# Rounded halves of Q and K loaded by a casting DMA of GpSimd in an attention and feed-forward kernel

## The chip, the cores and the metric

The kernel runs on one core of a Trainium2 chip. The metric is the time of one execution on the device, in microseconds (us). The engines are TensorE (PE; its weight loads are listed as PEld), VectorE (DVE), ScalarE (ACT), GpSimd (POOL) and SyncE (SP, which here only issues DMAs). Each engine runs its own instruction list strictly in order. An instruction that waits for a semaphore holds back all that stands behind it on that engine.

## The reference, cut to what matters

```python
# q, k, v: (8, 8, 576, 64) float32; f: (8, 8, 576)
scores = (1 / sqrt(64)) * q @ k.T
cum = cumsum(log(clip(f, 1e-4, 1)), axis=-1)
decay = cum[:, :, :, None] - cum[:, :, None, :]
attn = softmax(where(causal, -1e9, scores + decay))
x = (attn @ v).transpose(0, 2, 1, 3).reshape(8 * 576, 512)
h = x @ w_in                                   # 512 -> 2048
g = maximum(h, 0) + alpha * minimum(h, 0)
out = g @ w_out                                # 2048 -> 512
```

There are eight batches of eight heads, then a feed-forward layer over 4608 tokens.

## The kernel before, in words

**Pairs.** Two heads of a batch are worked on together, one in partitions 0 to 63 and one in 64 to 127. That makes 32 pairs, numbered n = 0 to 31, four to a batch. For each pair TensorE makes scores in tiles of 128 rows; VectorE adds the decay and the mask (tile `Z`, and `Zt` for the last 64 rows) and takes the row minimum of the negated scores; ScalarE takes the exponential; TensorE transposes the result (line 507), and then multiplies it by the values `vr`. The quotients go through `R`, `rd` and `ri`; VectorE multiplies (line 688), ScalarE rounds the product into `xx` (line 690), and GpSimd puts the remainder beside it (line 692).

**Split numbers.** The TensorE works here on numbers rounded to a shorter format (FP32R). To keep precision, a float32 operand is split into a rounded high half and a low half, the remainder, and a product becomes three products: high by high, high by low, low by high. From pair 4 on (`NN = 4`), Q and K are split so: `load_n` loads `rq` and `rk` (lines 423 and 424, issued by SP), ScalarE copies each to `Qh` and `Kh` (line 462; the write rounds), and GpSimd subtracts, `Ql = rq - Qh` and `Kl = rk - Kh` (line 463). The four halves lie in one buffer of the ring `rQ`, of which there are two. A buffer comes free when the scores of its pair are done, so the halves of pair n can be made once the scores of pair n - 2 are through. Pairs 0 to 3 use the whole float32 numbers.

**What else GpSimd does.** For each pair it prepares `Z` and `Zt` (lines 437, 438, 439, 454) after their loads, and it makes the low halves of `xx` (line 692) and, in the first 160 us, of the 16 columns of `w_in` (line 318, two instructions for each column, which is called fc 0 to fc 15 here). ScalarE (lines 305 and 317) and VectorE (lines 308 to 313) make the high halves of those columns.

**The first matrix product of the feed-forward layer** (`ffn1`) runs between the attention work. For each batch there are 16 columns, each with two halves of six products `bank<-xx,wi`. The first half of a column needs `xx` of the batch's pairs 0 and 1, the second half that of its pairs 2 and 3. The second product of the layer begins after all of it, at about 700 us.

**What sets the order.** The program order on each engine is found when the kernel is built, by a planner (`Plan.run`): each operation is given an engine, an assumed duration, a key and its dependencies. Again and again the planner takes the operation that can start earliest by its own clock, and among those of one engine the one with the lower key. An operation on the engine "-" takes time but no engine. The chip then runs the lists as they are: a wrong assumption shows as a wait. `o_scan` is the prefix sum at about 6 us; `dq` is empty for pair 0 and `[o_scan]` for the others; `kl` and `kc` are keys, the first lower.

Of the kernel before, what the change touches and what calls it, by code (L numbers as in the profile page):

```python
# [13 lines left out]
AF = mybir.ActivationFunctionType  # L14
# [3 lines left out]
B, H, S, D = 8, 8, 576, 64  # L18
# [5 lines left out]
QW = 640  # L24
# [58 lines left out]
class Plan:  # L83
# [5 lines left out]
    def op(self, eng, ns, fn, key, deps=(), bufs=(), two=False, kb=0.0):  # L89
        o = Op()  # L90
        o.eng, o.ns, o.fn, o.key, o.bufs, o.two, o.kb = eng, ns / 1000.0 * SLACK.get(eng, 1.0), fn, key, bufs, two, kb
        o.outs, o.ready, o.end, o.n = [], 0.0, None, 0
        for b in bufs:
            b.left += 1
        for d in deps:
            if d is not None and d.end is None:
                d.outs.append(o)
                o.n += 1
            elif d is not None:
                o.ready = max(o.ready, d.end + self.lag(d, o))  # L100
        self.ops.append(o)
        return o
# [83 lines left out]
def attention_moe(  # L186
# [14 lines left out]
    pe, ve, ac, po, sy = nc.tensor, nc.vector, nc.scalar, nc.gpsimd, nc.sync  # L201
# [3 lines left out]
    op = plan.op  # L205
# [63 lines left out]
    def c_mm(n):  # L269
        return max(110, 13.3 + 0.4175 * n)  # L270
# [7 lines left out]
    def c_act(n):  # L278
        return 65 + n / 1.2

    def c_acs(n):
        return 115 + n / 1.2
# [10 lines left out]
    def c_po(n):  # L293
        return 60 + 2.3 * n
# [26 lines left out]
    def mm(o, lhsT, rhs, start, stop):  # L321
        pe.matmul(o, lhsT, rhs, start=start, stop=stop)  # L322
# [92 lines left out]
    def load_n(n, held):  # L415

        b, p = divmod(n, NP)
        first = n == 0
        kl, kc, bh = NS * n - 16, NS * n - 7, b * H + 2 * p
        bq, bk, bZ = Buf(rrq), Buf(rrk), Buf(rZ)  # L420
        kq = -99 if first else -59 if n == 1 else kl
        dq = [] if first else [o_scan]
        l_q = op("SP", 450, lambda: sy.dma_start(bq.t, qq[b, p]), kq, dq, [bq], kb=320)
        l_k = op("SP", 450, lambda: sy.dma_start(bk.t, kk[b, p]), kq, dq, [bk], kb=288)
        Z, Zt = (lambda: bZ.t[0]), (lambda: bZ.t[1])
        rz = []
        for h in range(2):
            if first:
                bz_ = Buf(rH)
                up = op("PE", 4 * c_mm(512), lambda h=h, bz_=bz_: mm(bz_.t, row()[:, h], ft()[:, 0:512], True, True), -60 + h, o_8 + [o_row], [bft, brow, bz_])  # L430
                got = [op("ACT", c_act(512), lambda h=h, bz_=bz_: ac.activation(Z()[:, h, 0:512], bz_.t, AF.Copy), -60, [up], [bz_, bZ])]
            else:
                got = [op("SP", 400, lambda h=h: sy.dma_start(Z()[:, h, 0:512], c8[bh + h : bh + h + 1, 0:512].broadcast_to([128, 512])),
                          kl + 1, [o_c8], [bZ], kb=256)]
            z4 = lambda h=h: Z()[:, h].rearrange("p (j s) -> p j s", s=128)
            tb = lambda k: tri.rearrange("p (k s) -> p k s", k=1).broadcast_to([128, k, 128])
            m1 = op("POOL", c_po(128 * 3), lambda z4=z4: po.tensor_tensor(z4()[:, 6:9], z4()[:, 0:3], tb(3), ALU.add), kc + 0.1, got + [o_mask], [bZ])  # L437
            m2 = op("POOL", c_po(128), lambda z4=z4: po.tensor_tensor(z4()[:, 3], z4()[:, 3], tri, ALU.add), kc + 0.2, got + [o_mask], [bZ])
            m3 = op("POOL", c_po(128) / 2, lambda z4=z4: po.tensor_copy(z4()[:, 4], z4()[:, 1]), kc + 0.2, got, [bZ])
            rz.append([m1, m2, m3])  # L440
        if first:
            bz2 = [Buf(rH), Buf(rH)]
            cut = ((0, 512), (512, S))

            def up2():
                for b_, (a0, a1) in zip(bz2, cut):
                    mm(b_.t[:, 0 : a1 - a0], row()[:, 2], ft()[:, a0:a1], True, True)

            up = op("PE", 4 * c_mm(512) + 440, up2, -58, o_8 + [o_row], [bft, brow] + bz2)
            tz = [op("ACT", c_act(a1 - a0), lambda b_=b_, a0=a0, a1=a1: ac.activation(Zt()[:, a0:a1], b_.t[:, 0 : a1 - a0], AF.Copy), -58, [up], [b_, bZ])  # L450
                  for b_, (a0, a1) in zip(bz2, cut)]
        else:
            tz = [op("SP", 400, lambda h=h: sy.dma_start(Zt()[64 * h : 64 * h + 64], c8[bh + h : bh + h + 1].broadcast_to([64, S])), kl + 1, [o_c8], [bZ], kb=147) for h in range(2)]
        rt = op("POOL", 260, lambda: po.tensor_tensor(Zt()[:, 512:576], Zt()[:, 512:576], tri2, ALU.add), kc + 0.3, tz + [o_mask], [bZ])
        if n < NN:
            held += [bq, bk]
            return [l_q, l_k], rz, rt, bZ, [(lambda: bq.t, lambda: bk.t)]
        bQ = Buf(rQ)
        Qh, Ql, Kh, Kl = ((lambda j=j: bQ.t[j]) for j in range(4))
        out = []  # L460
        for hi, lo, raw, ld, w in ((Qh, Ql, bq, l_q, QW), (Kh, Kl, bk, l_k, S)):
            o1 = op("ACT", c_acs(w), lambda hi=hi, raw=raw: ac.activation(hi(), raw.t, AF.Copy), kc, [ld], [raw, bQ])  # L462
            o2 = op("POOL", c_po(w), lambda hi=hi, lo=lo, raw=raw: po.tensor_tensor(lo(), raw.t, hi().bitcast(F32), ALU.subtract), kc, [o1], [raw, bQ])  # L463
            out += [o1, o2]
        held.append(bQ)
        return out, rz, rt, bZ, [(Qh, Kh), (Qh, Kl), (Ql, Kh)]
# [3 lines left out]
    def attention(n):  # L470
# [6 lines left out]

        held = []
        rdy, rz, rt, bZ, terms = load_n(n, held)
        bv = Buf(rvr)  # L480
        l_v = op("SP", 400, lambda: sy.dma_start(bv.t, vv[b, p]), kl + 1, [o_scan], [bv], kb=320)
# [361 lines left out]
    for c in (0, 2):  # L843
        bt_ = Buf(rhr)
        tv = lambda bt_=bt_: bt_.t.rearrange("p c j t -> p c (j t)")
        ld = op("SP", 400, lambda c=c, tv=tv: sy.dma_start(tv(), xt[c : c + 2].rearrange("c p t -> p c t")), 1e6, [o_change] + xt_ops, [bt_], kb=512)
# [228 lines left out]
```

## Time and profile before

| | |
|---|---|
| median of 3 runs | 1083.31 us (1081.6 to 1084.06) |
| the profiled execution | 1082.03 us |
| its span, first to last instruction | 1080.2 us |
| mean granted TensorE clock | 0.997 |
| DVE busy | 707.3 us (65%) |
| ACT busy | 699.5 us (65%) |
| POOL busy | 279.4 us (26%) |
| moved by DMA | 170.57 MB, mean 158 GB/s |

The lines of the trace give a start and a duration in us, then the engine, the line of the kernel, the operation, its output and inputs by the names of their buffers with the partitions and elements, and a count where several are merged. In square brackets stands how long the engine was idle just before, and what ended that. SPq is the DMA queue of SP. Matmuls are pipelined and their ends are modelled.

### The profile page before, as it was taken

To read this page: it belongs to the slowest core of one execution; us is meant where nothing else is said; L and a number is where in the kernel's file an instruction comes from. 1 tells how busy PE (TensorE), PEld (TensorE's weight loads), DVE (VectorE), ACT (ScalarE), POOL (GpSimd) and SP (SyncE) were. 2 spreads that over 40 slices of the span, in tenths; PEclk is the share of its full clock that TensorE was granted. 3 is DMA by queue.
4 is the path that set the end of the run, shared out by engine and by line. 5 is a ranking of instruction groups with operands and counts; after the bars stand their busy time and mean duration, and the time that the engine had idled before them with its cause. 6 is when DMAs were issued, how large, how long until landed. Compare 5 with 4: busy or idle time off the path is not lost.

```text
span 1080.2 us, 20892 instructions
## 1 busy us (share of the span) xinstructions
PE 1068.2 (99%) x7428; PEld 910.8 (84%) x7428; DVE 707.3 (65%) x1632; ACT 699.5 (65%) x1638; POOL 279.4 (26%) x407
## 2 busy tenths in 40 slices
PE   8899999999999999999999999999999999999998
PEld 4577777777777777777787888899999999999998
DVE  6896745434434434434433497879989898989994
ACT  6898888967857857857846376656454554646551
POOL 6596774542443433433401000000000000000000
PEclk9999999999999999999999999999999999999999
DMA  6877766663653663553531566563433533443511
GB/s 184 252 221 239 241 193 180 191 182 115 184 174 118 179 181 115 177 177 115 151 104 71 166 221 233 193 206 117 150 126 118 157 118 120 139 134 125 147 61 39
DMA packets 116337, 170.57 MB, mean 158 GB/s; under 512 B 16626, under 2 KB 62601, under 8 KB 116233
## 3 DMA queue, kind: packets, MB, share of 16 engines
q1 hardware_dynamic: 115945, 169.05, 50.2%
q8 instruction: 58, 0.95, 0.4%
q14 instruction: 46, 0.38, 0.1%
q10 hardware_dynamic: 288, 0.20, 0.1%
HBM read 120.68 MB, written 48.52 MB: 157 GB/s over the span
## 4 chain that ended last, share of the span: by engine, by line
PE 96%; DVE 1%; DMA 1%; ACT 0%; POOL 0%; issue 0%; DVEq 0%
PE bank L322 87%; PE bank L507 8%; DMA wr<-in_w_in_dram 1%; PE bank L382 1%; DMA Zt<-c 0%; PE bank L646 0%; PE bank L571 0%; DVE xs L688 0%; ACT es L494 0%; DVE wa L313 0%; POOL Z L437 0%; DVE wa L312 0%; DVE e L527 0%; DVE eT L502 0%; DVE es L624 0%
## 5 line engine op out<-in xcount | busy, mean ns | idle before, releaser
L322 PE MATMUL bank<-xx,wi 128*128 128x512 f32 x1728 | 421.3, 396 | 0.3 <-DVE st L624 0.3
L322 PEld LDWEIGHTS bank<-xx,wi 128*128 128x128 f32 x1728 | 316.7, 188 | 63.3 <-issue 1.9
L770 DVE SCALAR_TENSOR_TENSOR hs<-bank,sa,hs 128x512 f32<-128x512 f32 x96 | 72.0, 750 | 156.6 <-ACT hs L768 156.6
L503 ACT ACTIVATE eT<-bank 128x384 f32<-128x384 f32 x240 | 109.2, 487 | 27.1 <-PE bank L507 23.7
L322 PE MATMUL bank<-wot,xx 128*128 128x256 f32 x1008 | 123.9, 284 | 0.0
L322 PE MATMUL bank<-wi,xx 128*128 128x256 f32 x1008 | 123.9, 284 | 0.0
L322 PEld LDWEIGHTS bank<-wi,xx 128*128 128x128 f32 x1008 | 122.3, 192 | 0.0
L322 PEld LDWEIGHTS bank<-wot,xx 128*128 128x128 f32 x1008 | 122.3, 192 | 0.0
L768 ACT ACTIVATE hs<-bank,ab 128x512 f32<-128x512 f32 x96 | 66.0, 687 | 81.0 <-PE bank L322 78.1
L494 ACT ACTIVATE e<-e,st 128x512 f32<-128x512 f32 (+2 forms) x160 | 109.1, 686 | 5.3 <-DVE st L527 3.4
L322 PE MATMUL bank<-eT,vr 128*64 128x320 f32 (+4 forms) x896 | 94.1, 360 | 0.0
L322 PEld LDWEIGHTS bank<-eT,vr 128*64 128x64 f32 x896 | 57.3, 137 | 40.8 <-issue 7.7
L507 PE MATMUL bank<-ident,e 128*128 128x128 f32 x576 | 87.9, 281 | 3.2 <-DVE st L624 1.6
L507 PEld LDWEIGHTS bank<-ident,e 128*128 128x128 f32 x576 | 68.2, 143 | 22.6 <-ACT e L494 6.0
L692 POOL TENSOR_TENSOR xx<-xs,xx 128x256 fp32r<-128x256 f32 x64 | 49.2, 785 | 146.7 <-ACT xx L690 146.7
L463 POOL TENSOR_TENSOR Ql<-rq,Qh 128x640 fp32r<-128x640 f32 x28 | 44.6, 1592 | 142.6 <-ACT Qh L462 57.8
L964 ACT ACTIVATE xx<-gx 128x1024 fp32r<-128x1024 f32 x48 | 50.8, 1058 | 30.8 <-PE bank L322 15.1
L437 POOL TENSOR_TENSOR Z<-Z,tri 128x384 f32<-128x384 f32 x64 | 61.9, 977 | 16.3 <-DMA Z<-c 8.8
L967 DVE TENSOR_TENSOR xx<-gx,xx 128x1024 fp32r<-128x1024 f32 x48 | 58.6, 1221 | 7.8 <-ACT xx L964 7.8
L322 PE MATMUL bank<-wi,gh 128*128 128x256 f32 x504 | 62.4, 284 | 0.0
L322 PE MATMUL bank<-wot,gh 128*128 128x256 f32 x504 | 62.4, 284 | 0.0
L322 PEld LDWEIGHTS bank<-wot,gh 128*128 128x128 f32 x504 | 61.4, 192 | 0.1
(137 smaller groups left out, 1690.0 us busy)
## 6 DMA issues: line engine op xcount, KB each, us to landing
hd<-hs SPq DMA_DIRECT2D x144, 256.0 KB, 2.0
wx<-hd SPq DMA_DIRECT2D x47, 512.0 KB, 4.1
Z<-c SPq DMA_DIRECT2D x62, 256.0 KB, 4.8
hr<-hd SPq DMA_DIRECT2D x25, 512.0 KB, 3.8
rq<-in_qq_dram SPq DMA_DIRECT2D x32, 320.0 KB, 5.3
vr<-in_vv_dram SPq DMA_DIRECT2D x32, 320.0 KB, 2.9
rk<-in_kk_dram SPq DMA_DIRECT2D x32, 288.0 KB, 3.4
Zt<-c SPq DMA_DIRECT2D x62, 144.0 KB, 5.0
```

The source lines that it names most:

```text
L322: pe.matmul(o, lhsT, rhs, start=start, stop=stop)
L382: op("PE", 800, lambda: [pe.matmul(bw.t, wbf[:, 0:128], wbf, start=True, stop=True) for _ in range(3)], -200, [o_wbf], [bw])
L437: m1 = op("POOL", c_po(128 * 3), lambda z4=z4: po.tensor_tensor(z4()[:, 6:9], z4()[:, 0:3], tb(3), ALU.add), kc + 0.1, got + [o_mask], [bZ])
L463: o2 = op("POOL", c_po(w), lambda hi=hi, lo=lo, raw=raw: po.tensor_tensor(lo(), raw.t, hi().bitcast(F32), ALU.subtract), kc, [o1], [raw, bQ])
L494: ex = op("ACT", c_exp(w), lambda: ac.activation(bt.t[:, :w], bt.t[:, :w], AF.Exp, bias=lo()[:, col : col + 1], scale=-1.0, accum_out=su() ...
L503: return op("ACT", c_act(w), lambda: ac.activation(dst(), src(), AF.Copy), key, deps, [bank] + bufs)
L507: pe.transpose(t[:, c : c + 128], src[:, 128 * j : 128 * j + 128], ident)
L692: xl = op("POOL", c_po(256), lambda r=r, t0=t0: po.tensor_tensor(bx.t[:, 1, t0 : t0 + 256], bxs[r].t[:, 0:256], bx.t[:, 0, t0 : t0 + 256]. ...
L768: cp = op("ACT", c_act(512), lambda bh=bh, bs=bs, fc=fc: ac.activation(bs.t, bh.t, AF.Relu, scale=ab[:, fc : fc + 1]), -1000, [last, o_sg] ...
L770: cp = op("DVE", c_dve(512), lambda bh=bh, bs=bs, fc=fc: ve.scalar_tensor_tensor(bs.t, bh.t, sa[:, fc : fc + 1], bs.t, ALU.mult, ALU.add), ...
L964: his.append(op("ACT", c_acs(128 * GW * (j1 - j0)), lambda j0=j0, j1=j1, src=src, o_=o_: ac.activation(o_(0, j0, j1), src(), AF.Copy), key ...
L967: rdy.append(op("DVE", c_dve(128 * GW * (j1 - j0)), lambda j0=j0, j1=j1, src=src, o_=o_: ve.tensor_tensor(o_(1, j0, j1), src(), o_(0, j0, ...
```

## The change

The rounded halves `Qh` and `Kh` are no longer copies by ScalarE. GpSimd issues a DMA from `qq` or `kk` in HBM to the tile, of another type than its source, so that the DMA converts. The planner is told 1100 ns of GpSimd for the issue and 3500 ns until the data are there; the subtraction waits for both that and the load of the raw numbers, which SP issues as before. The DMA has the key `kl + 2` in place of `kc`. It doesn't need the raw numbers, so it can stand earlier than the copy did. Everything else that moves is moved by the planner.

```diff
-        for hi, lo, raw, ld, w in ((Qh, Ql, bq, l_q, QW), (Kh, Kl, bk, l_k, S)):
-            o1 = op("ACT", c_acs(w), lambda hi=hi, raw=raw: ac.activation(hi(), raw.t, AF.Copy), kc, [ld], [raw, bQ])
+        for hi, lo, raw, ld, w, src in ((Qh, Ql, bq, l_q, QW, qq), (Kh, Kl, bk, l_k, S, kk)):
+            o1 = op("POOL", 1100, lambda hi=hi, src=src: po.dma_start(hi(), src[b, p]), kl + 2, dq, [bQ])
+            o1 = op("-", 3500, lambda: None, kl + 2, [o1, ld])
             o2 = op("POOL", c_po(w), lambda hi=hi, lo=lo, raw=raw: po.tensor_tensor(lo(), raw.t, hi().bitcast(F32), ALU.subtract), kc, [o1], [raw, bQ])
```

ScalarE has 56 instructions fewer, two for each of the 28 pairs from 4 on, and GpSimd has 56 DMAs more. Lines from 463 on are numbered one higher after the change, and the DMA stands in line 462.

**The start of GpSimd's list.** Here are the rows from the end of the constants (the selection rows in `e_124`) to the masks of pair 0 and the first of pair 1, before:

```order
L374 AFFINE_SELECT e_124<-e_124 64x64
L437 TENSOR_TENSOR Z_105<-Z_105,tri 128x384 x2
L438 TENSOR_TENSOR Z_105<-Z_105,tri 128x128
L439 COPY Z_105<-Z_105 128x128
L438 TENSOR_TENSOR Z_105<-Z_105,tri 128x128
L439 COPY Z_105<-Z_105 128x128
L454 TENSOR_TENSOR Zt_106<-Zt_106,tri_146 128x64
L437 TENSOR_TENSOR Z_107<-Z_107,tri 128x384
```

and the same place after the change (`Qh_93` and `Kh_95` are the first buffer of the ring, for pair 4; `Qh_97` and `Kh_99` the second, for pair 5):

```order
L374 AFFINE_SELECT e_124<-e_124 64x64
L462 DMA Qh_93<-in_qq_dram 128x640
L462 DMA Kh_95<-in_kk_dram 128x576
L462 DMA Qh_97<-in_qq_dram 128x640
L437 TENSOR_TENSOR Z_105<-Z_105,tri 128x384 x2
L438 TENSOR_TENSOR Z_105<-Z_105,tri 128x128
L439 COPY Z_105<-Z_105 128x128
L438 TENSOR_TENSOR Z_105<-Z_105,tri 128x128
L439 COPY Z_105<-Z_105 128x128
L454 TENSOR_TENSOR Zt_106<-Zt_106,tri_146 128x64
L462 DMA Kh_99<-in_kk_dram 128x576
L437 TENSOR_TENSOR Z_107<-Z_107,tri 128x384 x2
```

Three of the four first DMAs stand ahead of the masks of pair 0, the fourth ahead of those of pair 1.

**GpSimd around the masks of pair 5.** Before, from the second mask of pair 5 (`Z_107`) to the low half of the column fc 4, with the low halves of `xx` of pair 3 between:

```order
L437 TENSOR_TENSOR Z_107<-Z_107,tri 128x384
L438 TENSOR_TENSOR Z_107<-Z_107,tri 128x128
L439 COPY Z_107<-Z_107 128x128
L438 TENSOR_TENSOR Z_107<-Z_107,tri 128x128
L692 TENSOR_TENSOR xx<-xs_1_135,xx 128x256
L692 TENSOR_TENSOR xx<-xs_1_137,xx 128x256
L439 COPY Z_107<-Z_107 128x128
L454 TENSOR_TENSOR Zt_108<-Zt_108,tri_146 128x64
L318 TENSOR_TENSOR wi<-wa_143,wi 128x256 x2
```

After the change, from the last mask of pair 5 to the subtraction for pair 6 (the rows with `xs_0` are pair 2, those with `xs_1` pair 3; the two pairs of `wi` rows are fc 3 and fc 4):

```order
L439 COPY Z_107<-Z_107 128x128
L454 TENSOR_TENSOR Zt_108<-Zt_108,tri_146 128x64
L318 TENSOR_TENSOR wi<-wa_143,wi 128x256 x2
L462 DMA Qh_93<-in_qq_dram 128x640
L462 DMA Kh_95<-in_kk_dram 128x576
L693 TENSOR_TENSOR xx<-xs_0_134,xx 128x256
L693 TENSOR_TENSOR xx<-xs_0_136,xx 128x256
L318 TENSOR_TENSOR wi<-wa_143,wi 128x256 x2
L693 TENSOR_TENSOR xx<-xs_1_135,xx 128x256
L693 TENSOR_TENSOR xx<-xs_1_137,xx 128x256
L464 TENSOR_TENSOR Ql_94<-rq_102,Qh_93 128x640
```

The low halves of `xx` of pairs 2 and 3 now stand behind all masks of pair 5, behind two DMAs for pair 6, and those of pair 3 behind fc 4 too.

**TensorE where the second half of column fc 0 needs them.** Before, from the transposes of pair 4 (`e_122`, `e_123`) to those of its last tile; `bank_82` is the first half of fc 1, `bank_81` the second half of fc 0:

```order
L507 MATMUL bank_80<-ident,e_125 128x128 x3
L646 MATMUL bank_80<-ident,e_122 64x128
L507 MATMUL bank_83<-ident,e_123 128x128 x3
L322 MATMUL bank_82<-xx,wi 128x512 x6
L322 MATMUL bank_81<-xx,wi 128x512 x6
L507 MATMUL bank_80<-ident,e_121 128x128 x4
L507 MATMUL bank_83<-ident,e_124 128x128 x4
```

After the change the first halves of fc 0 (`bank_76`) and fc 1 (`bank_83`) stand together, ahead of pair 4's transposes, behind the products with the values of pair 3:

```order
L322 MATMUL bank_80<-eT_2_113,vr_110 64x128
L322 MATMUL bank_80<-eT_3_114,vr_110 64x128
L322 MATMUL bank_76<-xx,wi 128x512 x6
L322 MATMUL bank_83<-xx,wi 128x512 x6
L508 MATMUL bank_79<-ident,es_128 128x128
L508 MATMUL bank_79<-ident,es_130 128x128 x2
```

and the second half of fc 0 (`bank_76`) stands directly behind the scores of pair 5:

```order
L322 MATMUL bank_82<-Kh_99,Ql_98 128x384
L322 MATMUL bank_79<-Kh_99,Ql_98 128x384
L322 MATMUL bank_76<-xx,wi 128x512 x6
L508 MATMUL bank_80<-ident,e_121 128x128 x4
L508 MATMUL bank_81<-ident,e_124 128x128 x4
L322 MATMUL bank_83<-xx,wi 128x512 x6
```

Between the first half of fc 0 and its second half there stand the same first half of fc 1, 17 of pair 4's transposes and the first 18 score products of pair 5, before and after; only their sequence differs.

## Prediction

> **What bounds the kernel now.** First the page's busy times and the chain that ended last.
>
> ```profile
> PE 1068.2 (99%) x7428; PEld 910.8 (84%) x7428; DVE 707.3 (65%) x1632; ACT 699.5 (65%) x1638; POOL 279.4 (26%) x407
> PE 96%; DVE 1%; DMA 1%; ACT 0%; POOL 0%; issue 0%; DVEq 0%
> ```
>
> TensorE is busy for 1068.2 of 1080.2 us, and 96% of the chain is TensorE. At most 12 us can be won without giving TensorE less work, and the change leaves its products as they are. Then by stages (columns: the stretch, its length, busy time of each engine with instructions, granted clock, DMA share, GB/s):
>
> ```profile
> core 0: us, PE busy (x) PEld busy (x) DVE busy (x) ACT busy (x) POOL busy (x), PEclk, DMA share, GB/s
> 0.00:60.00 60.00, 52.71 (x321) 32.51 (x321) 45.20 (x139) 45.88 (x133) 37.66 (x79) 0.94 0.75 221
> 60.00:80.00 20.00, 19.71 (x138) 16.24 (x139) 18.60 (x41) 17.65 (x53) 18.31 (x23) 1.00 0.73 213
> 80.00:160.00 80.00, 80.00 (x552) 61.59 (x551) 52.20 (x139) 71.42 (x190) 55.80 (x70) 1.00 0.72 227
> 160.00:590.00 430.00, 429.30 (x2840) 336.29 (x2839) 183.84 (x581) 307.08 (x833) 164.54 (x233) 1.00 0.49 152
> 590.00:1080.20 490.20, 486.43 (x3584) 464.12 (x3582) 407.45 (x735) 257.45 (x434) 3.08 (x4) 1.00 0.45 142
> ```
>
> TensorE's idle time is 7.3 us before 60, 0.3 to 80, none from 80 to 160, 0.7 to 590 and 3.8 at the end. So a ScalarE that is 89% busy from 80 to 160 (71.42 of 80) holds nobody up there: relief of it can be worth something only before 60 us. GpSimd, at 26% of the whole, is 92% busy from 60 to 80 (18.31 of 20). That is where work added to it is felt.
>
> **What goes: ScalarE's copies.**
>
> ```profile
> L462 ACT ACTIVATE Qh<-rq 128x640 fp32r<-128x640 f32 x28 | 20.4, 730 | 0.0
> L462 ACT ACTIVATE Kh<-rk 128x576 fp32r<-128x576 f32 x28 | 18.8, 672 | 0.0
> ```
>
> 28 x 0.730 + 28 x 0.672 = 39.3 us leave ScalarE, 24 of the 28 pairs in stretches where TensorE never waits. The order shows them gone, so the change does what it says there. Before 60 us the copies stand near two waits of TensorE:
>
> ```profile
> 43.65 0.72 ACT L462 ACTIVATE Qh<-rq 128x640 fp32r<-128x640 f32 x1
> 51.56 1.50 PE L322 MATMUL bank<-rk,rq 64*128 64x512 f32 x2 [2.62 <-DVE st L527]
> 59.23 0.66 PE L507 MATMUL bank<-ident,e 128*128 128x128 f32 x4 [0.69 <-ACT e L494]
> ```
>
> The wait at 51.56 is for VectorE's pass over `Zt` of pair 3, behind a load, not for ScalarE; what is late there stays late. The 0.7 us at 59.23 could shrink. I count 0, bounds 0 and -2.1 (0.7 and one pair of copies, 1.4).
>
> **What comes: the price of an issue on GpSimd.** No DMA of GpSimd is in the trace. The nearest rows are SP's issue of the same transfer, short and long, and GpSimd's own pass over such a tile.
>
> ```profile
> 14.13 0.34 SPq L423 DMA_DIRECT2D rq<-in_qq_dram  x1
> 1.40 0.56 SPq L423 DMA_DIRECT2D rq<-in_qq_dram  x1
> L463 POOL TENSOR_TENSOR Ql<-rq,Qh 128x640 fp32r<-128x640 f32 x28 | 44.6, 1592 | 142.6 <-ACT Qh L462 57.8 <-DMA Z<-c 42.3 <-issue 15.4
> ```
>
> Bounds 0.34 and 1.59 us. [...]
>
> **First term, the start.** Three of the DMAs stand ahead of pair 0's masks.
>
> ```profile
> 7.74 0.91 POOL L374 TENSOR_SCALAR_AFFINE_SELECT e<-e 64x128 f32<-64x128 f32 x4
> 10.67 1.78 POOL L437 TENSOR_TENSOR Z<-Z,tri 128x384 f32<-128x384 f32 x2 [2.03 <-ACT Z L431]
> 11.61 0.29 DVE L624 CUSTOM_DVE_ANT_0 es<-bank,Z 128x128 f32<-128x128 f32 x1 [4.58 <-POOL Z L437]
> ```
>
> GpSimd is free at 8.65 and waits 2.0 us for ScalarE; 3 x 1.1 = 3.3 us fill that and put the masks 1.3 us late. VectorE waits for them (4.58 us) and TensorE for VectorE, so the whole start shifts: **+1.3 us** (0 at 0.34 or 0.56 each, 2.7 at 1.59). The fourth, ahead of pair 1's masks, delays nothing that is due.
>
> **Second term, `xx` of pair 3.** Around 70 us the trace shows, on TensorE, the first half of fc 0 at 65.81, and six products of fc 1 followed by fc 0's second half at 70.64:
>
> ```profile
> 65.81 1.66 PE L322 MATMUL bank<-xx,wi 128*128 128x512 f32 x6 [0.28 <-DVE st L624]
> 69.94 2.33 POOL L692 TENSOR_TENSOR xx<-xs,xx 128x256 fp32r<-128x256 f32 x2
> 70.64 3.00 PE L322 MATMUL bank<-xx,wi 128*128 128x512 f32 x12
> 72.21 0.76 POOL L439 COPY Z<-Z 128x128 f32<-128x128 f32 x1
> 72.94 0.30 POOL L454 TENSOR_TENSOR Zt<-Zt,tri 128x64 f32<-128x64 f32 x1
> 73.63 1.42 POOL L318 TENSOR_TENSOR wi<-wa,wi 128x256 fp32r<-128x256 f32 x2 [0.39 <-ACT wi L317]
> ```
>
> Twelve products take 3.00 us, 0.25 each, so fc 0's second half starts at 70.64 + 1.50 = 72.1, and its fifth product, the first that reads pair 3's low half, at 73.1. GpSimd delivers that at 69.94 + 2.33 = 72.3, a margin of 0.8 us. By the order, TensorE arrives at the same point after the change, since between the halves of fc 0 stand the same instructions. GpSimd arrives later by what now stands ahead: the copy 0.76, `Zt` 0.30, fc 4 1.42, and two DMAs 2.2, in sum 4.7 us. TensorE, in order, waits 4.7 - 0.8 = **+3.9 us**; transposes and scores of pair 5's rest are queued behind it. Bounds: 4.7 becomes 3.2 with issues of 0.34, 5.7 with 1.59; GpSimd could use up to its 1.7 us of idle time in the stretch, and a load may come earlier: 0.5 to 4.9.
>
> **80 to 160 us.** Here I count 0. Five pairs are scored there, so 10 issues, 11 us, and GpSimd is idle for 24.2 us. Part of that idle time was waiting for the copies:
>
> ```profile
> POOL Ql L463 <- ACT Qh L462: 8.6, 3, 3.2
> POOL Kl L463 <- ACT Kh L462: 4.9, 2, 3.5
> rq<-in_qq_dram SPq DMA_DIRECT2D x32, 320.0 KB, 5.3
> rk<-in_kk_dram SPq DMA_DIRECT2D x32, 288.0 KB, 3.4
> ```
>
> In place of 13.5 us (from 76 to 156 us) comes waiting for the DMA. If it lands like SP's, in 5.3 us, and some 2.5 us of other work (the second issue and one `wi` pair) lie between, a pair waits 2.8 us, 14 us in all. 11 + 14 = 25 us into 24.2: just full, nothing over. TensorE's lateness from the first terms gives some 5 us more room.
>
> **From 160 us.** One pair in the steady state, the last score product of pair 19 and the first of pair 21 around its copy:
>
> ```profile
> 339.24 0.39 PE L322 MATMUL bank<-Kh,Ql 64*128 64x512 f32 x2
> 345.78 0.72 ACT L462 ACTIVATE Qh<-rq 128x640 fp32r<-128x640 f32 x1
> 359.36 0.33 PE L322 MATMUL bank<-Kh,Qh 64*128 64x128 f32 x2
> ```
>
> The buffer is free at 339.6 and read at 359.4, 19.7 us later. Two issues (2.2), a landing of 5.3 from the first issue's end (1.1 of it beside the second), the two passes (1.6 and 1.5, from the page) and masks of some 2 fit in 11.5; there are 8 us over. **0**, up to a landing of 13 us.
>
> **Sum.** 1.3 + 3.9 = 5.2 us on the profiled execution's 1082.0: 1087.2. The median of the runs shown lies 1.3 us above that execution, which would make 1088.5; I give **1088**.
>
> **Rivals.**
> - *Hidden after all, 1084* (25%). With 0.34 us an issue, as on SP, the start costs nothing and the second term falls to 0.5 to 1.5. For it: GpSimd still has 1.7 us of idle time there, and ScalarE's relief may bring `wi` and `xx` earlier. Against: the order alone puts 2.5 us of other work ahead.
> - *Faster, 1080.5* (17%). ScalarE is the place: its exponentials near 45 and 59 us move up by a pair of copies each and take 2.1 us from TensorE's 7.3 us of idle time, with issues so short that nothing is paid. It decides from issues under 0.6 us and if pair 3's `xx` comes in time. Against: the long wait, 2.62 us, is ended by VectorE behind a load.
> - *Slow landing, 1096* (13%). The conversion or the shared DMA engines (share 0.72 from 80 to 160) make a landing of 8 us in place of 5.3: five pairs wait 2.7 us longer each, 13.5 us more on a GpSimd that is full, `wi` of the late columns comes late, and after some 5 us of room TensorE stands for about 8 us. It decides from a landing of about 6.3 us.
> [...]
>
> [...]
>
> **How the numbers follow.** The forecast has 37%, and with the two slow rivals 58% for slower. A measurement of this kernel tells about 0.2%, 2.2 us, from no change: slower is above 1085.5, faster below 1081.1. Hidden is 25% for no change, the faster rival 17%. The forecast's own bounds are 1083 to 1091 (terms 0 + 0.5 and 2.7 + 4.9, and the 1.3 us between execution and median). For 8 in 10 the range reaches into both sides, 1080 to 1097, and leaves out the end of the fast rival and what a landing over 8 us would make.
>
> **What would show it.** The first mask of pair 0 at about 12 instead of 10.67 us; a wait of TensorE of about 4 us at fc 0's second half near 73 us, ended by GpSimd's `xx`; GpSimd's `Ql` waiting for a DMA instead of ScalarE; no waits of TensorE from 160 us on. A mask at 10.7 would make the price of an issue wrong, a second half without wait the second term, and waits of TensorE for `wi` from 80 to 160 us the assumed landing.

## The result, and the profile after

| | before | after |
|---|---|---|
| median | 1082.77 us of 4 runs (1081.60 to 1084.06) | 1092.52 us of 4 runs (1090.26 to 1094.14) |
| profiled execution, its span | 1082.03 us, 1080.2 us | 1091.89 us, 1090.1 us |
| mean granted TensorE clock | 0.997 | 0.993 |

The kernel became slower by the ratio 1.0088, with a 95% interval of 1.0066 to 1.0111, some 9.7 us. The page of the kernel after has in its first part the busy times and in its fourth the chain that ended last:

```profile
PE 1071.6 (98%) x7428; PEld 910.5 (84%) x7428; DVE 709.9 (65%) x1632; ACT 667.7 (61%) x1582; POOL 311.3 (29%) x463
PE 93%; DMA 2%; DVE 2%; POOL 2%; issue 0%; ACT 0%; SPq 0%; DVEq 0%; POOLq 0%
```

ScalarE has lost 31.8 us (699.5 to 667.7) and GpSimd has gained 31.9 us, and TensorE, with the same 7428 matmuls, is busy for 3.4 us longer and is a smaller part of the chain. By stages (the columns are those of the prediction's table), the kernel after:

```profile
0.00:60.00 60.00, 53.23 (x321) 32.29 (x321) 41.19 (x134) 42.49 (x127) 38.38 (x82) 0.94 0.86 241
60.00:80.00 20.00, 14.92 (x96) 10.47 (x96) 14.94 (x32) 10.98 (x33) 14.29 (x21) 0.83 0.74 214
80.00:160.00 80.00, 77.42 (x519) 59.82 (x517) 60.36 (x145) 63.93 (x176) 57.32 (x72) 1.00 0.84 236
160.00:590.00 430.00, 429.79 (x2848) 336.36 (x2846) 183.02 (x583) 287.15 (x801) 198.23 (x288) 1.00 0.63 186
```

TensorE's idle time is 6.8, 5.1, 2.6 and 0.2 us in these stretches; before it was 7.3, 0.3, 0 and 0.7. That is 6.4 us more, and it comes from the stretch of 60 to 160 us. The two spans differ by 9.9 us; the rest is TensorE's busy time, which is 3.4 us longer. Most of that is the granted clock. From 60 to 80 us it fell from 1.00 to 0.83, which is 0.17 x 20 = 3.4 us of full speed, but about a third of this fell into time in which TensorE stood anyway, so that some 2.3 us of work were lost (the windows are in the last section). Where the last microsecond of busy time lies isn't shown.

**The first stop.** The timeline of the kernel after, from 59 to 68 us, of VectorE and TensorE:

```profile
60.93 1.12 DVE L308 TENSOR_SCALAR wa<-wr 128x512 uint32<-128x512 uint32 x1 [0.27 <-POOL wi L318]
...
64.74 1.28 DVE L313 SCALAR_TENSOR_TENSOR wa<-wi,wa 128x512 f32<-128x512 f32 x1
65.94 0.45 DVE L528 CUSTOM_DVE_ANT_0 e<-bank,Zt 128x288 f32<-128x288 f32 x1
...
61.87 1.55 PE L322 MATMUL bank<-R,sel 9*128 9x128 f32 x12 [1.93 <-ACT R L573]
...
67.13 5.08 PE L322 MATMUL bank<-eT,vr 128*64 128x320 f32 x28 [2.81 <-DVE st L528]
```

VectorE makes the column fc 3 of `w_in` (lines 308 to 313) from 60.9 to 66.0, and only then reduces pair 4's tail, its last 64 rows (line 528). TensorE needs that, since the value products of pair 3 go into the two banks in which the tail's scores wait: it stands for 2.81 us at 67.13, after 1.93 us for `R` a little earlier. Before, the same instructions stood so:

```profile
59.30 0.45 DVE L527 CUSTOM_DVE_ANT_0 e<-bank,Zt 128x288 f32<-128x288 f32 x1
61.87 0.41 DVE L308 TENSOR_SCALAR wa<-wr 128x512 uint32<-128x512 uint32 x1
...
61.06 2.99 PE L322 MATMUL bank<-eT,vr 128*64 128x320 f32 x28
63.98 1.55 PE L322 MATMUL bank<-R,sel 9*128 9x128 f32 x12
```

VectorE reduced the tail first and made the column after it, and TensorE made the products of `R` behind the value products, without a wait. So the planner moved two things on engines that the change doesn't touch. On VectorE fc 3's pass went ahead of the tail (rows without their numbers, before and after; Zt_106 is pair 4's):

```
L624 ISA es_126,st_132<-bank_79,Z_105 128x256
L527 ISA e_122,st_132<-bank_82,Zt_106 128x288
L527 ISA e_122,st_132<-bank_83,Zt_106,st_132 128x288
L308 TENSOR_SCALAR wa_143<-wr_142 128x512

L625 ISA es_126,st_132<-bank_77,Z_105 128x256
L308 TENSOR_SCALAR wa_143<-wr_142 128x512
L528 ISA e_122,st_132<-bank_80,Zt_106 128x288
L528 ISA e_122,st_132<-bank_79,Zt_106,st_132 128x288
```

(each piece leaves out the rows between that both have). On TensorE the products of `R` went from behind 6 score products and the value products to a place right behind the transpose of `st` that feeds them.

The place of fc 3's pass isn't all of the first stop. The four instructions took 5.1 us there (60.93 to 66.02), where they took 3.4 us before (61.87 to 65.29); fc 4's four, at 68.46 in the kernel after, are 2.5 us in sum. GpSimd worked on masks and on `Kl` beside the first and mostly stood beside the last. No run varies this, so what stretched the pass stays open.

**The second stop.** GpSimd's low half of fc 4 comes late, VectorE's pass for fc 5 waits 3.75 us for the one-buffer `wa`, and with it what stands behind it:

```profile
77.02 1.42 POOL L318 TENSOR_TENSOR wi<-wa,wi 128x256 fp32r<-128x256 f32 x2 [2.22 <-ACT wi L317]
78.47 0.94 DVE L308 TENSOR_SCALAR wa<-wr 128x512 uint32<-128x512 uint32 x1 [3.75 <-POOL wi L318]
...
85.25 0.28 PE L572 MATMUL bank<-ident,st 128*9 128x128 f32 x1 [1.50 <-DVE st L625]
```

**The DMAs themselves.** The view of line 462 (minimum, median and maximum of one issue in ns), the page's DMA issues (KB each, median us from issue to landing), and the list of waits (total, times, longest):

```profile
L462 POOL DMA_DIRECT2D Qh<-in_qq_dram x28: 535/573/697, 8.6 to 540.5; - x28
L462 POOL DMA_DIRECT2D Kh<-in_kk_dram x28: 527/535/631, 9.3 to 541.1; - x28
Qh<-in_qq_dram POOLq DMA_DIRECT2D x28, 320.0 KB, 4.0
Kh<-in_kk_dram POOLq DMA_DIRECT2D x28, 288.0 KB, 4.7
POOL Ql L464 <- DMA Qh<-in_qq_dram: 65.2, 22, 4.6
POOL Kl L464 <- DMA Kh<-in_kk_dram: 0.9, 1, 0.9
```

An issue takes 0.53 to 0.70 us and lands after a median of 4.0 and 4.7 us. GpSimd's `Ql` now waits for the DMA instead of ScalarE, in all 65.2 us, and no matmul of TensorE in this kernel waits for GpSimd (one weight load does, 0.3 us for `Kl`).

### The profile page after: what moved, and what is told of

Read it like the earlier page. It is cut to its first block, busy times and chain, and to the rows that moved or that the text cites. A ratio compares the mean times of both kernels' runs of the same rounds, so it can differ in the third digit from the quotient of the medians.

```text
span 1090.1 us, 20921 instructions
## 1 busy us (share of the span) xinstructions
PE 1071.6 (98%) x7428; PEld 910.5 (84%) x7428; DVE 709.9 (65%) x1632; ACT 667.7 (61%) x1582; POOL 311.3 (29%) x463
## 4 chain that ended last, share of the span: by engine, by line
PE 93%; DMA 2%; DVE 2%; POOL 2%; issue 0%; ACT 0%; SPq 0%; DVEq 0%; POOLq 0%
PE bank L322 85%; PE bank L508 7%; DMA Zt<-c 1%; DMA wr<-in_w_in_dram 1%; POOL wi L318 0%; DVE wa L312 0%; DVE wa L308 0%; POOL Z L437 0%; PE bank L572 0%; PE bank L647 0%; DMA e<-in_f_dram 0%; DVE wa L309 0%; POOL Z L438 0%; POOL Z L439 0%; DVE wa L313 0%
## 5 line engine op out<-in xcount | busy, mean ns | idle before, releaser
L322 PE MATMUL bank<-xx,wi 128*128 128x512 f32 x1728 | 423.0, 396 | 1.0 <-DVE st L625 1.0
L322 PEld LDWEIGHTS bank<-xx,wi 128*128 128x128 f32 x1728 | 316.0, 188 | 66.1 <-issue 3.8
L322 PE MATMUL bank<-wot,xx 128*128 128x256 f32 x1008 | 123.9, 283 | 0.0
L322 PE MATMUL bank<-wi,xx 128*128 128x256 f32 x1008 | 123.9, 283 | 0.0
L322 PEld LDWEIGHTS bank<-wot,xx 128*128 128x128 f32 x1008 | 122.3, 192 | 0.0
L322 PEld LDWEIGHTS bank<-wi,xx 128*128 128x128 f32 x1008 | 122.3, 192 | 0.0
L322 PE MATMUL bank<-eT,vr 128*64 128x320 f32 (+4 forms) x896 | 96.5, 366 | 3.5 <-DVE st L528 2.8
L322 PEld LDWEIGHTS bank<-eT,vr 128*64 128x64 f32 x896 | 57.3, 139 | 47.1 <-issue 7.7
L508 PE MATMUL bank<-ident,e 128*128 128x128 f32 x576 | 84.1, 280 | 2.7 <-DVE st L625 1.2
L495 ACT ACTIVATE es<-es,st 128x256 f32<-128x256 f32 (+1 forms) x128 | 57.0, 449 | 10.5 <-DVE st L625 10.3
L464 POOL TENSOR_TENSOR Ql<-rq,Qh 128x640 fp32r<-128x640 f32 x28 | 44.1, 1574 | 65.2 <-DMA Qh<-in_qq_dram 65.2
L322 PE MATMUL bank<-wi,gh 128*128 128x256 f32 x504 | 62.4, 283 | 0.0
L322 PE MATMUL bank<-wot,gh 128*128 128x256 f32 x504 | 62.4, 283 | 0.0
```

The costliest lines, as they stand in the source:

```text
L495: ex = op("ACT", c_exp(w), lambda: ac.activation(bt.t[:, :w], bt.t[:, :w], AF.Exp, bias=lo()[:, col : col + 1], scale=-1.0, accum_out=su() ...
L508: pe.transpose(t[:, c : c + 128], src[:, 128 * j : 128 * j + 128], ident)
```

## The experiments

In the first four, theory 1 says that the new order of the early part costs the time and the DMA itself nothing; theory 2 says that the DMA's issue and landing cost it, and theory 3 its traffic. Theories A to D are in the texts of the later ones.

### The DMA in the old order

The plan of the kernel before, in which only the function of ScalarE's copy is exchanged; VectorE and TensorE keep their lists, and on GpSimd each DMA stands where the copy was planned, mostly right ahead of its subtraction (0 to 6 rows between).

```diff
-            o1 = op("ACT", c_acs(w), lambda hi=hi, raw=raw: ac.activation(hi(), raw.t, AF.Copy), kc, [ld], [raw, bQ])
+            o1 = op("ACT", c_acs(w), lambda hi=hi, src=src: po.dma_start(hi(), src[b, p]), kc, [ld], [raw, bQ])
```

> TensorE's and VectorE's lists are those of the kernel before; the casting DMA stands on GpSimd where ScalarE's copy was planned, right ahead of its subtraction. Theory 1 (the new order of the first 100 us costs the time): 1083 to 1086 us, TensorE idle at most 0.5 us from 60 to 160 us. Theory 2 (GpSimd's issues and its waits for the landing cost it): 1092 us or more, since here each subtraction waits some 4 us right behind its DMA. Theory 3 (the 17.4 MB more of DMA slow the loads): 1086 to 1092 us.

Measured 1136.01 us, ratio 1.05 (1.0475 to 1.0526): by itself a point for theory 2 and a miss of theory 1's 1083 to 1086. Its list of waits:

```profile
POOL Kl L463 <- DMA Kh<-in_kk_dram: 74.0, 22, 6.2
POOL Ql L463 <- DMA Qh<-in_qq_dram: 39.0, 11, 6.2
```

GpSimd stands through 113 us of landings, and all that is queued behind them on it comes late. So the DMA isn't free wherever it stands; it needs the early place that the key `kl + 2` gives it. There a pair's two DMAs mostly stand together, issued as the buffer comes free (at 318.69 and 319.30 us, for one pair), so that one wait covers both landings: `Ql` waits 65.2 us in all and `Kl` 0.9, and TensorE takes up that pair only at 341.06. In the old order the DMA of `Kh` mostly comes later (302.20 for `Qh`, 312.35 for `Kh`), with a landing of its own.

### The new order without the DMA

The plan of the kernel after; GpSimd's issue does nothing, and ScalarE copies as before. VectorE and TensorE have the lists of the kernel after.

```diff
-            o1 = op("POOL", 1100, lambda hi=hi, src=src: po.dma_start(hi(), src[b, p]), kl + 2, dq, [bQ])
-            o1 = op("-", 3500, lambda: None, kl + 2, [o1, ld])
+            o1 = op("POOL", 1100, lambda: None, kl + 2, dq, [bQ])
+            o1 = op("-", 3500, lambda hi=hi, raw=raw: ac.activation(hi(), raw.t, AF.Copy), kl + 2, [o1, ld], [raw, bQ])
```

> TensorE's and VectorE's lists are those of the changed kernel, but the halves are copies by ScalarE and there is no casting DMA; the planner still counts 1100 ns of GpSimd and 3500 ns of landing. Theory 1 (order): 1090 to 1095 us, with the same stop of TensorE between 59 and 67 us. Theory 2 (issue and landing) and theory 3 (DMA traffic): 1083 to 1085 us.

Measured 1090.8 us, ratio 1.0069 (1.0048 to 1.009). The timeline of TensorE has the same two waits:

```profile
62.25 1.55 PE L322 MATMUL bank<-R,sel 9*128 9x128 f32 x12 [1.93 <-ACT R L573]
67.95 4.48 PE L322 MATMUL bank<-eT,vr 128*64 128x320 f32 x28 [3.02 <-DVE st L528]
```

The order alone, with no DMA of GpSimd, makes most of the loss. What the DMA adds to it, 1.7 us by the medians, lies within the overlap of the two intervals.

### The DMA from pair 12 on, and up to pair 11

```diff
+            if n >= 12:
+                o1 = op("POOL", 1100, lambda hi=hi, src=src: po.dma_start(hi(), src[b, p]), kl + 2, dq, [bQ])
+                o1 = op("-", 3500, lambda: None, kl + 2, [o1, ld])
+            else:
+                o1 = op("ACT", c_acs(w), lambda hi=hi, raw=raw: ac.activation(hi(), raw.t, AF.Copy), kc, [ld], [raw, bQ])
```

and the same with `n < 12`.

> Copies by ScalarE for pairs 4 to 11, casting DMAs for pairs 12 to 31; the order is that of the kernel before up to about 150 us. Theory 1 (order of the first 100 us): 1083 to 1085 us, since the steady state has room for a landing of 4 us. Theory 2 (issue and landing): 20 of 28 pairs pay, 1089 us. Theory 3 (traffic): 1086 to 1089 us.

> Casting DMAs for pairs 4 to 11 only, copies by ScalarE from pair 12 on; the order is that of the changed kernel up to about 170 us. Theory 1 (order of the first 100 us): 1090 to 1094 us, all of the loss. Theory 2: 8 of 28 pairs pay, 1086 us. Theory 3: 1085 to 1088 us.

Measured 1081.80 us, 0.9998 (0.9988 to 1.0008), and 1092.22 us, 1.0092 (1.0076 to 1.0107). All of the loss belongs to the pairs below 12. In the steady state TensorE is busy to the hundredth as before, with 429.30 of 430 us from 160 to 590:

```profile
160.00:590.00 430.00, 429.30 (x2841) 336.13 (x2840) 183.89 (x581) 285.86 (x795) 188.03 (x274) 1.00 0.60 180
```

### A second buffer for `wa`

The order of the kernel after; fc 1, fc 3 and fc 5 work in a tile of `hs` that is not yet in use.

```diff
+        turn.append(0)
+        spare = len(turn) in (2, 4, 6)
-        a = lambda: shape(ba.t)
+        a = lambda: shape(hs[:, 3].bitcast(U32)) if spare else shape(ba.t)
```

> The order of the kernel after on every engine, but the passes of the columns fc 1, fc 3 and fc 5 work in a spare tile in place of the one-buffer wa, so VectorE's passes no longer wait for GpSimd's wi. Theory A (at the first stop the place of fc 3's pass ahead of pair 4's tail costs, not its wait of 0.27 us; the wait of 3.75 us for wa at 78 us makes the second stop): the first stop stays, TensorE's value products still begin near 66.5, the second stop of 1.5 us goes: 1089 to 1091.5 us beside 1092.5. Theory B (the single wa is the whole cause): 1083 to 1086. Theory C (GpSimd being full costs, by masks and low halves, not VectorE's passes): 1092 to 1093.

Measured 1088.81 us, 1.005 (1.0031 to 1.0068), just under the range of theory A (by 0.2 us), 2.8 us above B's and 3.2 under C's. In its timeline fc 5's pass starts without a wait, and TensorE's second stop is gone:

```profile
75.29 0.42 DVE L311 TENSOR_SCALAR hs<-wr 128x512 uint32<-128x512 uint32 x1
67.64 4.48 PE L325 MATMUL bank<-eT,vr 128*64 128x320 f32 x28 [0.35 <-DVE st L531]
```

The value products still begin at 67.64. The wait in front of them is short because TensorE comes later to it: in this execution it began the scores ahead of them at 65.64, 2.3 us later than in the kernel after. On the way there it had stood 1.79 us for GpSimd's `Kl` at 55.29, a wait that the kernel after doesn't have.

### One move on VectorE, and its mirror

From here on some kernels take a recorded order instead of the planner's search, with the named rows moved; all other rows of all engines stay. Their files are longer, so line numbers are higher (L626 there is L322 here). In the kernel after, fc 3's pass goes behind pair 4's tail (ScalarE's copy of the column behind the tail's exponential):

```diff
-L308 TENSOR_SCALAR wa_143<-wr_142 128x512
-L309 SCALAR_TENSOR_TENSOR wa_143<-wr_142,wa_143 128x512
-L312 SCALAR_TENSOR_TENSOR wa_143<-wr_142,wa_143 128x512
-L313 SCALAR_TENSOR_TENSOR wa_143<-wi,wa_143 128x512
 L528 ISA e_122,st_132<-bank_80,Zt_106 128x288
 L528 ISA e_122,st_132<-bank_79,Zt_106,st_132 128x288
+L308 TENSOR_SCALAR wa_143<-wr_142 128x512
+L309 SCALAR_TENSOR_TENSOR wa_143<-wr_142,wa_143 128x512
+L312 SCALAR_TENSOR_TENSOR wa_143<-wr_142,wa_143 128x512
+L313 SCALAR_TENSOR_TENSOR wa_143<-wi,wa_143 128x512
```

and in the kernel before, which has no DMA of GpSimd, the same four rows, and ScalarE's copy with them, go the other way.

> The order of the kernel after with one move: VectorE's four instructions over wa for fc 3 stand behind the two reductions of pair 4's tail instead of ahead of them, and ScalarE's copy of that column behind the tail's exponential. The DMAs stay. Theory A: the tail is reduced at 60.8 instead of 65.9, the stop of 2.8 us at 67 us goes, the value products begin near 63 to 64, and 3 to 6 of the 10 us are got back: 1086.5 to 1089.5. If all of the loss hangs on this one place: 1083 to 1085. Theory C: no change, 1092 to 1093.

> The kernel before, with ScalarE's copies and without the casting DMA, and with the opposite move alone: fc 3's pass on VectorE stands ahead of the two reductions of pair 4's tail, and ScalarE's copy of the column ahead of the tail's exponential. Theory A: VectorE waits for wa until 61.3, the tail is reduced near 65.5 instead of 59.3, TensorE stops near 61 us, and the kernel before becomes slower by 3 to 7 us: 1086 to 1090. Theory C: under 1.5 us slower, 1082 to 1084.

Measured 1088.46 us, 1.0051 (1.0032 to 1.007), and 1089.09 us, 1.0055 (1.0034 to 1.0076). The move gives back some 4 us of the kernel after, and its mirror alone takes 6 to 7 us from the kernel before. The mirror's profile has one long new stop, and from 60 to 80 us:

```profile
65.75 0.38 PE L872 MATMUL bank<-ident,st 128*9 128x128 f32 x1 [4.86 <-DVE st L870]
60.00:80.00 20.00, 15.12 (x99) 10.48 (x98) 13.07 (x40) 11.62 (x38) 10.72 (x16) 0.83 0.64 185
```

Idle time from 60 to 80 us goes from 0.3 to 4.9, and the clock from 1.00 to 0.83: 4.6 us and at most 3.4, since a little of the slow time lies over the stop, where the spans differ by 8.2 (1088.4 and 1080.2). That these rows in a wrong place can make 6 to 7 us of loss, with no DMA at all, is shown. In the kernel after, the opposite move doesn't take away the wait for `R`, which stands ahead of it, nor the second stop:

```profile
59.50 2.67 PE L626 MATMUL bank<-R,sel 9*128 9x128 f32 x12 [1.93 <-ACT R L877]
...
81.05 0.28 PE L876 MATMUL bank<-ident,st 128*9 128x128 f32 x1 [1.51 <-DVE st L929]
```

### The planner told the measured prices

```diff
-            o1 = op("POOL", 1100, lambda hi=hi, src=src: po.dma_start(hi(), src[b, p]), kl + 2, dq, [bQ])
-            o1 = op("-", 3500, lambda: None, kl + 2, [o1, ld])
+            o1 = op("POOL", 570, lambda hi=hi, src=src: po.dma_start(hi(), src[b, p]), kl + 2, dq, [bQ])
+            o1 = op("-", 4000, lambda: None, kl + 2, [o1, ld])
```

> The kernel after, but the planner is told the measured prices, 570 ns for an issue and 4000 ns until the data are there, instead of 1100 and 3500, and makes its own order. In that order fc 3's pass still stands ahead of pair 4's tail. Theory A (what stands where decides, and this place is as in the kernel after): 1088 to 1094. Theory D (the false price sent the planner astray): 1082 to 1085.

Measured 1085.53 us, 1.0027 (1.0015 to 1.0039): better than theory A said, not as good as D. Its profile:

```profile
64.64 4.88 PE L322 MATMUL bank<-eT,vr 128*64 128x320 f32 x28 [3.01 <-DVE st L528]
80.00:160.00 80.00, 80.00 (x539) 62.15 (x538) 58.03 (x137) 65.59 (x181) 56.63 (x74) 1.00 0.82 245
```

(The second row is the stretch from 80 to 160 us.) The stop for pair 4's tail is there, as theory A said, but 2.5 us earlier than in the kernel after, and there is no second stop. So some 7 of the 10 us hung on two numbers that the planner was told, by way of the order that it made of them.

### Combinations, and a control

Four kernels: both edits in the kernel after; the order with the measured prices, with the move on VectorE; that with the second buffer too; and the kernel before with the second buffer alone. Their edits are those above.

> The kernel after with both edits: fc 3's pass on VectorE behind the reductions of pair 4's tail, and the passes of fc 1, fc 3 and fc 5 in a spare tile. Alone they gave back 4.0 and 3.7 us. Theory A (two stops, each with its own link): the gains add, the second stop of 1.5 us near 81 us goes too, 1084 to 1086. Rival (both edits cure the same stop): 1087.5 to 1089.

> The order that the planner makes with the measured prices (the run before that got 1085.5), with one move: fc 3's pass on VectorE behind the reductions of pair 4's tail. There TensorE still stopped for 3.0 us at 64.6, ended by that tail. Theory A: this stop goes, 1082 to 1083.5. Rival (the stop only hides another wait, for GpSimd's low halves or the copies of the exponentials): 1084.5 to 1086.

> The kernel of the run before this, and the passes of fc 1, fc 3 and fc 5 in a spare tile. Theory A: no stop of that kind is left after 60 us, so 0 to 1 us less than the run before it: 1081 to 1083. If the casting DMA brings anything once the order is mended, this run shows it: below 1080. Rival: no difference between the two.

> The control: the kernel before, with ScalarE's copies, and with the passes of fc 1, fc 3 and fc 5 in the spare tile. In the kernel before VectorE waits little for wa and TensorE is idle for 0.3 us from 60 to 160 us, so by all theories no change: 1081.5 to 1083. Should it be faster by 2 us or more, what the spare tile gave back in the kernel after was not a repair of what the change did.

Measured 1088.91 us (1.0053, 1.0038 to 1.0067), 1085.09 us (1.0025, 1.0015 to 1.0034), 1083.87 us (1.001, 1.0001 to 1.0018) and 1082.19 us (0.9997, 0.9987 to 1.0007). The control agrees: the spare tile does nothing for the kernel before. The other three are misses of theory A, which had each repaired stop pay in full; of the rivals, those of the first two hold the measured times (1087.5 to 1089 and 1084.5 to 1086). Their timelines show where it went, of the first and of the second:

```profile
170.53 0.40 PE L629 MATMUL bank<-Kh,Qh 128*128 128x288 f32 x1 [1.65 <-ACT xs L984]
```

```profile
59.67 1.89 PE L626 MATMUL bank<-R,sel 9*128 9x128 f32 x12 [1.93 <-ACT R L877]
80.04 0.27 PE L876 MATMUL bank<-ident,st 128*9 128x128 f32 x1 [1.23 <-ACT wi L621]
```

With both edits TensorE has no second stop, so the two stops aren't one, as that rival had it; but it stands at 170.5 for ScalarE's `xs`, where it stood neither in the kernel before nor in the kernel after. With the measured prices the tail's stop is gone, but a new one of 1.23 us comes at 80 us, and the 1.93 us for `R` stay. The third has neither of the stops of VectorE; by stages, and with its longest wait:

```profile
0.00:60.00 60.00, 51.79 (x321) 31.56 (x321) 42.82 (x140) 44.04 (x134) 39.86 (x84) 0.97 0.91 254
60.00:80.00 20.00, 19.56 (x119) 14.51 (x120) 17.34 (x37) 13.28 (x38) 17.39 (x21) 0.83 0.66 190
80.00:160.00 80.00, 79.24 (x531) 61.29 (x532) 56.42 (x137) 65.16 (x178) 54.96 (x72) 1.00 0.81 242
53.23 0.33 PE L629 MATMUL bank<-Kl,Qh 64*128 64x128 f32 x2 [2.73 <-POOL Kl L771]
```

TensorE is idle there for 8.2 + 0.4 + 0.8 us, 1.1 us more than before up to 590 us (9.4 and 8.3), and the clock costs 1.8 + 3.4 us where it cost 3.6 before, 1.6 more: 2.7 us, and the spans differ by 3.1. The wait of 2.73 us for `Kl` of pair 4 is one that GpSimd's list makes: GpSimd had stood 4.19 us for the load of a mask until 47.51, and `Kl` comes behind that mask, `xx` and a column. No version was faster than the kernel before. That the rest hangs on this wait and on that for `R` (1.93 us at 60.36), with the clock behind them, is read from these lines alone; a kernel that puts the products of `R` back behind the value products wasn't tried, so it stays open.

## Why the prediction came near, and where it was wrong

**The size came out, the sum behind it didn't.** Predicted were 1088 us in a range of 1080 to 1097, and slower as the likeliest sign; measured were 1092.5. That the time lies so near is luck: with an issue of 0.55 us, as measured, the prediction's own sum is 0 at the start and 0.76 + 0.30 + 1.42 + 2 x 0.55 - 0.8 = 2.8 us at `xx`, where the spans differ by 9.9. Term by term:

- **The price of an issue** was taken as 1.1 us, the author's estimate within the bounds of 0.34 and 1.59. No run shows it: the 56 issues took 0.53 to 0.70 us, at the lower bound's side, near SP's long issue of 0.56. The landing was taken as 5.3 us; its medians are 4.0 and 4.7.
- **The start, +1.3 us: wrong, about 0.** The sign that the prediction named did appear, but it is no proof:

```profile
11.80 1.78 POOL L437 TENSOR_TENSOR Z<-Z,tri 128x384 f32<-128x384 f32 x2 [1.45 <-ACT Z L431]
11.92 1.78 POOL L738 TENSOR_TENSOR Z<-Z,tri 128x384 f32<-128x384 f32 x2 [3.27 <-ACT Z L732]
```

  The first row is the kernel after, where GpSimd, with its three DMAs done, still waits 1.45 us for ScalarE. The second is the mirror experiment, which has no DMA on GpSimd and whose mask is just as late. In the six kernels that have no DMA ahead of this mask it starts between 10.67 and 12.11 us.
- **The second term, +3.9 us at GpSimd's `xx`: right stretch, right kind, wrong link.** The prediction said that the planner's new order would make TensorE wait near 73 us. It did make it wait, from 60 to 85 us. But `xx` of pair 3 held up nobody. This is the second half of fc 0 in the kernel after:

```profile
79.43 1.66 PE L322 MATMUL bank<-xx,wi 128*128 128x512 f32 x6
```

  It has no wait. GpSimd delivered the low half of pair 3 at 80.0 us in place of 72.3, 7.7 us later where the prediction had 4.7. But TensorE, already stopped twice, began these products at 79.43 in place of 72.1, and it needs that half only for the fifth of them, near 80.4. The step that failed is the comparison of the orders. It followed GpSimd's list, the engine that is given work, and compared TensorE's list only between the halves of fc 0. VectorE's rows around pair 4's tail, four rows that changed places, and the products of `R` weren't looked at.
- **From 80 to 160 us, 0: wrong by 2.6 us of idle time**, not through the landing, as the rival had it; 1.5 us of it are the second stop, through `wa`.
- **From 160 us, 0: right**, as the DMA from pair 12 on shows (0.9998).
- **ScalarE's relief, 0: right.** 31.8 us less of busy time on it (the prediction counted 39.3 us of copies) brought nothing that the intervals can tell from the new order with ScalarE's copies (1.0088 and 1.0069).
- **The clock wasn't in the sum at all.** It makes some 2.3 of the 9.9 us.
- **The fast rival** named two conditions, issues under 0.6 us and `xx` of pair 3 in time. Both came about (medians 0.57 and 0.54 us, no wait at 79.43), and the kernel was slower all the same: of TensorE's 7.3 us of idle time before 60 us, 6.8 stayed. The slow landing didn't come about (medians of 4.0 and 4.7 us, where it needed about 6.3).
- **Issues held up by VectorE** were the second slow rival, with 8%. That they would be was the author's estimate, and no run shows it: the longest of the 56 issues took 0.70 us, and one beside a pass over `wa`, at 68.38 us, took 0.63 where the median of its kind is 0.57.

## What to carry to other kernels

Where a planner makes the order, a small edit is first of all a new order on every engine: compare the lists of the engines that the edit doesn't touch, around each place where the bounding engine has no slack, before pricing the edit itself. A transfer that replaces a copy, issued by the engine that uses it, needs its issue early enough that this engine's wait for the landing ends before others need it; in the copies' old places the same DMAs cost 53 us. And repairing one stop pays only up to the next one, so a repair is judged by the end of the kernel and not by the stop that went.

## What the runs showed of the hardware

In some stretches of these runs, of about 3.4 and 6.8 us, the granted clock of TensorE was 0.50. They began behind or in a stop, and such a stop cost more than its length, by 1.7 and 2.2 us as worked out below. The windows of the kernel before from 18 to 22 and from 52 to 56 us, of the kernel after from 64 to 72, and of the order with the measured prices and the move on VectorE from 80 to 82 (length, TensorE busy, granted clock, DMA share, GB/s):

```profile
18.00:22.00 4.00, 4.00 (x16) 0.57 0.49 162
52.00:54.00 2.00, 1.99 (x7) 0.55 0.76 260
54.00:56.00 2.00, 2.00 (x12) 0.60 0.94 317
```

```profile
64.00:66.00 2.00, 0.32 (x4) 0.68 0.60 127
66.00:68.00 2.00, 0.87 (x4) 0.50 0.71 213
68.00:70.00 2.00, 2.00 (x10) 0.50 0.47 132
70.00:72.00 2.00, 2.00 (x20) 0.62 0.97 297
```

```profile
80.00:82.00 2.00, 1.96 (x11) 1.00 1.01 354
```

Where a window lies wholly in the slow time its clock is 0.50, so a window's time at half clock is taken as twice what its clock lacks of 1.00. That is 0.43 x 4 x 2 = 3.4 us in the first, (0.45 + 0.40) x 2 x 2 = 3.4 us in the second and (0.32 + 0.50 + 0.50 + 0.38) x 2 x 2 = 6.8 us in the third, which is the kernel after. In the first two TensorE was busy throughout, so each cost 1.7 us. The third began before the stop was over, and only busy time counts: 0.87 x 0.50 + 2 x 0.50 + 2 x 0.38 = 2.2 us, and up to 0.1 before 64.3. The value products at 67.13 took 5.08 us where the same 28 took 2.99 before.

The first follows a wait of 1.62 us at 17.35, the second that of 2.62 at 51.56; the third follows that of 1.93 at 61.87 and began in that of 2.81. Behind the single waits of 1.50 us at 85.25 in the kernel after, and of 1.23 at 80.04 in the order with the measured prices and the move on VectorE, the clock stayed at 1.00. In the kernel with the DMA from pair 12 on the first two of these waits, each ended by the same pass of VectorE as in the kernel before, are 1.6 and 2.1 us. Its mean clock up to 60 us is 0.97 where that of the kernel before is 0.94: in the same way 0.03 x 60 x 2 = 3.6 us at half clock in place of some 7. So one of the two went without a slow stretch, and what decides that these runs don't show.
